# Five w2T tiles in flight, a third w1 column block loaded early, bias transposes moved and inverse tables split by engine, in a spectral mixer and token MLP with its backward pass

## The chip, the cores and the metric

The kernel runs on one core of a Trainium2 chip. A core has TensorE (PE, matmul; its weight loads are listed as PEld), VectorE (DVE), ScalarE (ACT), GpSimd (POOL) and SyncE (SP), which here issues every DMA. The metric is device time in microseconds (us). Before the change it is 399.45 us, the median of three runs (397.94 to 399.71).

## The reference

One block of a network is computed forward, and then the gradients of its output with respect to seven inputs. S = 2048 tokens, D = 448 channels, F = 1792 hidden units, bfloat16:

```
A(x)  = irfft2( rfft2(x) * (w_r + i w_i) )              # over tokens and channels
B(x)  = ( gelu( layernorm(x)^T @ w1 + b1 ) @ w2 + b2 )^T  # mixes tokens
h     = x + A(layernorm(x))
out_0 = h + B(layernorm(h))
out_1..out_7 = gradients of x, w_r, w_i, w1, b1, w2, b2 for a given grad_out
```

## The kernel before

The transforms are matmuls with tables of sines and cosines. The forward part has these stages, in the order of the trace.

**Row stage** (the loop over t in NT = 16). Block t of tokens is transformed over the channels: row_a and row_b are eight matmuls each time, with copies between them by ScalarE or VectorE. A reshape DMA (L632, one for each t, deferred by a little TensorE time) brings each result into D2, in the layout that the transform over tokens needs. Meanwhile VectorE and ScalarE build the token tables Ut and Vt from small columns made on POOL (gen_UV), and the spectral weights come in through eight row loads (w_load, L559).

**s2 stage** (s2_stage). After all sixteen reshapes VectorE negates a part of D2, and then eight column groups c2 are transformed over the tokens, multiplied by the spectral weights on VectorE (w_mult, four operations for each group) and transformed back (s2_inv). The multiplication of group c2 is emitted four steps after its transform, and the transform back two steps later still. The results go through reshape DMAs (L698) into D3. The inverse tables over channels, csI, are made by gen_inv_d, one half at the end of the row stage and one half at c2 = 1; those over tokens by gen_inv_s.

**dg filler**. A quite different product, grad_out times the transposed w2 (dg_gen, 14 tiles of 16 matmuls), is spread over the row and s2 stages to fill TensorE: fill(n) runs n of its matmuls. Each of its tiles needs a w2T tile, 512 KB, brought in by a transposing DMA (load_w2T, L292). The ring of w2T tiles has five places, three in rE and two in rO. Three tiles are loaded at the start, and when a dg tile ends, the load three tiles ahead is issued. While hold is set (from t = 2*HOLD = 14 to the start of s2) these loads are put aside and then issued at the first step of s2.

**Inverse rows** (inv_rows with h_consumer). The transform back over channels, the sum h in region rA, and its layernorm. At its end h is stored to DRAM (L926).

**GELU stage** (the loop over jp). Seven column blocks of w1, 256 columns each, are multiplied with the normalised h; GELU and its derivative follow, most of it on VectorE. The blocks come from load_w1c (L867) into a ring of three places: two in region r2, one in rA. Two are loaded before the inverse rows. The third is loaded after the h store, which reads rA.

**y stage and after**. y = gelu @ w2 with column blocks of w2 (load_w2c, L913), output (y_tail), and then the backward pass, which the change does not touch.

All orders on TensorE, ScalarE, VectorE and SyncE are the order in which the program emits instructions; POOL's are arranged by a scheduler. SyncE issues its DMAs one after the other, so each waits for the issue of all before it. Copies out of PSUM (evac) go to ScalarE or VectorE by a running count of the load of both. The bias loads put b1 and b2 into rows of smr; `turn`, deferred by 15 us of TensorE time, turns them into columns with two transposing DMAs (L759), and POOL copies them into b1col and b2col (L760). Most instructions are recorded under L78 (ScalarE and VectorE) and L212 (matmul), so the profile is read by tile names.

Of the kernel before, what the change touches and what calls it, by code (L numbers as in the profile page):

```python
# [13 lines left out]
ALU = mybir.AluOpType  # L14
# [4 lines left out]
S = 2048  # L19
# [4 lines left out]
NFB = 14  # L24
NT = 16
# [9 lines left out]
RESH_LAG = 1.1  # L35
ML_F = 4
SIDE = 2
HOLD = 7
N_FILL_F = (6, 3, 20, 3, 24, 2)
N_FILL_B = (16, 16, 40, 8, 32, 12)  # L40
INV_SD = 1.0 / float(S * D)

# [76 lines left out]
def kernel(  # L119
# [37 lines left out]
    def cut(reg, off, *dims):  # L157
        n = int(np.prod(dims))
        v = reg[:, off:off + n]
        if len(dims) == 1:  # L160
            return v
        names = "abcd"[:len(dims)]
        return v.rearrange("p (" + " ".join(names) + ") -> p " + " ".join(names),
                           **{c: d for c, d in zip(names, dims)})
# [5 lines left out]
    def ps_ff(parts=P):  # L170
        return psum.tile([P, 512], F32, tag="ff", bufs=4, name="ps_ff")
# [24 lines left out]
    def defer(us, fn, *views):  # L196
        state = [fn]

        def run():
            if state:  # L200
                state.pop()()
        later.append((clock[0] + us, len(later), run))
        later.sort(key=lambda x: x[0])
        for v in views:
            Ring.held.setdefault(id(v), []).append(run)
# [43 lines left out]
    def col(n=1):  # L249
        i = _ci[0]  # L250
        _ci[0] += n
        assert _ci[0] <= 64
        return cols[:, i:i + n]
# [33 lines left out]
    def load_w2T():  # L287
        j = w2T_ring.i
        if j == NFB:
            return  # L290
        wT = w2T_ring.next()
        nc.sync.dma_start_transpose(out=wT, in_=B_w2[j * P:(j + 1) * P, :].rearrange("f (t c) -> f t c", c=P))  # L292
        w2Ts.append(wT)
# [208 lines left out]
            mm(pt[:, i * P:(i + 1) * P], lhsT=src[:, g0 + i, :], rhs=permI[:], start=True, stop=True)  # L502
        evac(out=dst[:, g0:g0 + 4, :].rearrange("p g c -> p (g c)"), in_=pt[:])

    def gen_inv_d(ch):
        e, en = col(), col()
        gp_.memset(e, 2.0)
        if ch == 0:
            gp_.memset(e[0:1, :], 1.0)
        else:  # L510
            ve.tensor_scalar(out=e, in0=pcol, scalar1=112.0, scalar2=None, op0=ALU.not_equal)
            ve.tensor_scalar(out=e, in0=e, scalar1=1.0, scalar2=None, op0=ALU.add)
            gp_.memset(e[0:1, :], 0.0)
        ve.tensor_scalar(out=en, in0=e, scalar1=-1.0, scalar2=None, op0=ALU.mult)
        gp_.tensor_scalar(out=halves[:, ch:ch + 1], in0=e, scalar1=-0.5, scalar2=1.5, op0=ALU.mult, op1=ALU.add)
        pt = ps_ff()[:].bitcast(BF16)[:, 0:2 * 2 * P].rearrange("p (w b c) -> p w b c", w=2, b=2)
        for w in range(2):
            for b in range(2):
                nc.tensor.transpose(pt[0:KC, w, b, :], csF[:, w, b, DC * ch:DC * ch + KC], ident[:])
        for w, x in ((0, e), (1, en)):  # L520
            for b in range(2):
                lo = D - DC - DC * b
                sc.activation(out=csI[0:KC, w, ch, DC * b:DC * b + DC], in_=pt[0:KC, w, b, 0:DC], func=ACT.Copy,
                              scale=e[0:KC])
                ve.tensor_scalar(out=csI[0:KC, w, ch, lo:lo + DC], in0=pt[0:KC, w, b, DC - 1::-1], scalar1=x[0:KC],
                                 scalar2=None, op0=ALU.mult)

    base = ftmp(3072, 16, 16, 2)
    fix = ftmp(3584, 16)
# [84 lines left out]
    def row_a(t, R):  # L614
        pa = ps_ff()
        ft = folds[t // 2]
        for k in range(4):
            o = DC * (4 * (t % 2) + k)
            mm(pa[:, k * P:(k + 1) * P], lhsT=ft[:, o:o + P], rhs=R, start=True, stop=True)
        blk = blk_ring.next()  # L620
        evac(out=blk.rearrange("p a b -> p (a b)"), in_=pa[:])
        return blk
# [11 lines left out]
    def s2_stage(get_x, on_mult, ml, n_fill, gap, make_inv, after_fwd=None, scale=None):  # L634
        flush()
        for c4 in range(4):
            ve.tensor_scalar(out=D2[:, 4 * c4:4 * c4 + 4, 2, :], in0=D2[:, 4 * c4:4 * c4 + 4, 0, :], scalar1=-1.0,
                             scalar2=None, op0=ALU.mult)
        nh = NG // 2
        xs, ys = {}, {}  # L640

        def g_last(c2, i):
            return after_fwd is not None and 2 * c2 + i == NG - 1
        lag = 2 + ml
        negs.clear()
        for c2 in range(nh + lag):
            if c2 < nh:
                xs[c2] = get_x(c2)
                if make_inv and c2 < 4:
                    gen_inv_s(4 + c2)  # L650
                    if c2 == 1:
                        gen_inv_d(0)
            for i in range(2):
                if make_inv:
                    next(wp, None)
                    next(wp, None)
                if c2 < nh:
                    g = 2 * c2 + i
                    px = ps_ff()
                    pv = px[:, 0:452].rearrange("p (c k) -> p c k", c=2)  # L660
                    mm(pv, lhsT=Ut[:, g, :], rhs=D2[:, g, 1:3, :], start=True, stop=False)
                    mm(pv, lhsT=Vt[:, g, :], rhs=D2[:, g, 0:2, :], start=False, stop=True)
                    evac(out=xs[c2][:, i, :, :], in_=pv, scale=scale)
                if c2 >= lag:
                    s2_inv(2 * (c2 - lag) + i, ys[c2 - lag][:, i, :, :])
                if g_last(c2, i):
                    after_fwd()
                while negs:
                    negs.pop(0)()
                fill(n_fill)  # L670
            if ml <= c2 < nh + ml:
                ys[c2 - ml] = on_mult(c2 - ml, xs[c2 - ml])
        fill(gap)
# [78 lines left out]
    def load_biases():  # L752
        gp_.memset(smr, 0.0)
        nc.sync.dma_start(out=smr[0:NFB, 0, :], in_=B_b1.rearrange("(j p) -> j p", p=P))
        nc.sync.dma_start(out=smr[:, 1, :], in_=B_b2.rearrange("(j p) -> j p", p=P))

        def turn():
            for i, dst in ((0, b1col), (1, b2col)):
                nc.sync.dma_start_transpose(out=smc[:, i, :], in_=smr[:, i, :])  # L759
                gp_.tensor_copy(out=dst[:], in_=smc[:, i, :])  # L760
        defer(15.0, turn)


    def dg_gen():
# [30 lines left out]
    weave(fwd_c[:2], [lambda: ve.reciprocal(out=rstd_x[:, 0:4], in_=rstd_x[:, 0:4])])  # L795
    Rs = {t: scale_R(t) for t in range(2)}
    weave(fwd_c[2:])
    gp_.memset(csF[:, 0, :, 0:1], 0.0)  # L798
    ve.tensor_scalar(out=ident[:], in0=krow[:, 0:P], scalar1=pcol, scalar2=None, op0=ALU.is_equal)
    gp_.memset(W_view_F[:, :, :, DF:KW], 0.0)  # L800
    w_loads = w_load()
    uv = gen_UV()
    blks = {0: row_a(0, Rs.pop(0))}
    fold_prep(xn, 1)
    for t in (4, 5):
        ln_stats(xn, t, mvx)
    fill(N_FILL_F[0])
    load_biases()
    Meter.side, Meter.every, Meter.count = [], 1, 0
    GROUPS = {0: (4, 8), 4: (8, 12), 8: (12, 16)}  # L810
    STATS = {0: (6, 7), **{t: (t + 7,) for t in range(1, 9)}}
    INV_S = {11: 0, 12: 1, 13: 2, 14: 3}
    sc.copy(out=Rp.rearrange("p (a q b) -> p a q b", q=8, a=4), in_=Rm[:].rearrange("p (q a b) -> p a q b", q=8, a=4))
    for t in range(NT):
        hold[0] = t >= 2 * HOLD
        if t + 1 < NT:
            blks[t + 1] = row_a(t + 1, Rs.pop(t + 1))
        fill(N_FILL_F[1])
        if t + 2 < NT:
            if t + 2 in (4, 8, 12):  # L820
                while Meter.side:
                    Meter.side.pop(0)()
            Rs[t + 2] = scale_R(t + 2)
        row_b(t, blks.pop(t))
        if t % 2 and t < 12:
            fold_prep(xn, t // 2 + 2)
        for i in STATS.get(t, ()):
            ln_stats(xn, i, mvx)
        for _ in range(3 if t > 0 else 0):
            if next(uv, None):  # L830
                break
        if t in GROUPS:
            Meter.side.extend(rstd_of(*GROUPS[t]))
        if t >= 3:
            next(w_loads, None)
        if t in INV_S:
            gen_inv_s(INV_S[t])
        if t == 2:
            gen_RT()
        if t == 15:  # L840
            gen_inv_d(1)
        fill(N_FILL_F[1])
# [7 lines left out]
    def fwd_x(c2):  # L850
        hold[0] = False
        while held_w2:
            held_w2.pop(0)()
        return Xs[:, 2 * c2:2 * c2 + 2, :, :]

    def fwd_mult(c2, xc):
        return w_mult(c2, xc, W_view_F, False)

    s2_stage(fwd_x, fwd_mult, ML_F, N_FILL_F[3], N_FILL_F[4], True)

    nc.sync.dma_start(out=w_d[:], in_=rG[:, 0:NG * 2 * KW])

    w1c_ring = Ring([cut(r, o, NT, 256) for r, o in ((r2, 0), (r2, NT * 256), (rA, 0))])

    def load_w1c(jp):
        w = w1c_ring.next()
        nc.sync.dma_start(out=w, in_=B_w1.rearrange("(p t) f -> p t f", t=NT)[:, :, 256 * jp:256 * jp + 256])  # L867
        return w

    w1cs = [load_w1c(0), load_w1c(1)]  # L870

    hn = xn
    hln = cut(rB, 0, NT, 4, P)[:, :, :, 0:DC]
# [31 lines left out]
            ve.tensor_scalar(out=hln[:, t, :, :], in0=v4(hn[:, t, :]), scalar1=nmean_h[:, t:t + 1],  # L905
                             scalar2=rstd_h[:, t:t + 1], op0=ALU.add, op1=ALU.mult)

    w2c_ring = Ring([cut(r, o, NFB, 256) for r, o in ((rS, 0), (rS, NFB * 256), (r452, 0), (rO, 0), (r2, NT * 256), (r2, 0))])
    w2cs = {}

    def load_w2c(i):
# [12 lines left out]
        norm_h(t, t == 14)  # L924
    drain()
    nc.sync.dma_start(out=h_d.rearrange("(p t) d -> p t d", t=NT), in_=hn)  # L926
    w1cs.append(load_w1c(2))

    g_ = cut(rE, 0, NFB, 4, P)[:, :, :, 0:DC]
    gel = [ring(rG, i * 4 * 896, 4, 2, D) for i in range(2)]  # L930
# [279 lines left out]
```

## Time and profile before

| | |
|---|---|
| median of the runs | 399.45 us (397.94, 399.45, 399.71) |
| the profiled execution, its own time | 402.57 us |
| its span, first to last instruction | 400.8 us |
| busy share PE, DVE, ACT, POOL | 90%, 71%, 52%, 6% |
| mean granted TensorE clock | 0.982 |
| moved by DMA | 81.86 MB, 204 GB/s over the span |
| row stage, about 10 to 54 us; s2, 58 to 92; inverse rows, 97 to 116 | |
| GELU stage, 116 to 172; y stage, 172 to 216; backward, from there | |

In the views, times are microseconds from the start of the span. A timeline line gives start, duration, engine, line, operation, destination<-source, and in brackets the idle time before it with what ended it. SyncE's lines are the issues of DMAs (SPq); the transfer itself runs on 16 DMA engines and ends later. Region names that end in digits are shortened by the profile (r2, r3 and r452 all appear as r), and the tensor names too: in_B_w_dram is w1 or w2 by the line. Matmuls of 128 x 448 follow each other every 0.19 us at full clock though each is listed with some 0.35 us, as they are pipelined.

### The profile page before, as it was taken

To read this page: it belongs to the slowest core of one execution; us is meant where nothing else is said; L and a number is where in the kernel's file an instruction comes from. 1 tells how busy PE (TensorE), PEld (TensorE's weight loads), DVE (VectorE), ACT (ScalarE), POOL (GpSimd) and SP (SyncE) were. 2 spreads that over 40 slices of the span, in tenths; PEclk is the share of its full clock that TensorE was granted. 3 is DMA by queue.
4 is the path that set the end of the run, shared out by engine and by line. 5 is a ranking of instruction groups with operands and counts; after the bars stand their busy time and mean duration, and the time that the engine had idled before them with its cause. 6 is when DMAs were issued, how large, how long until landed. Compare 5 with 4: busy or idle time off the path is not lost.

```text
span 400.8 us, 6200 instructions
## 1 busy us (share of the span) xinstructions
PE 360.8 (90%) x2057; PEld 191.5 (48%) x2057; DVE 285.0 (71%) x729; ACT 207.0 (52%) x439; POOL 22.9 (6%) x92
## 2 busy tenths in 40 slices
PE   0798789988996999999999999899999889799995
PEld 0464535534643455545555666543444335455552
DVE  8979457982876588843249787737999924779784
ACT  4486455674976254414213444535545525667772
POOL 8500000000220000000030000000000000000000
PEclk9999988999999899999999999999999999999999
DMA  8979788167996999687958894596555989966775
GB/s 214 312 161 202 166 188 183 39 148 250 297 343 171 306 331 242 170 253 192 198 121 164 176 180 105 94 289 198 167 158 161 216 256 312 252 193 174 190 189 207
DMA packets 148297, 81.86 MB, mean 204 GB/s; under 512 B 97448, under 2 KB 142504, under 8 KB 147880
## 3 DMA queue, kind: packets, MB, share of 16 engines
q1 hardware_dynamic: 148264, 81.46, 80.2%
q8 instruction: 16, 0.26, 0.3%
q14 instruction: 17, 0.14, 0.1%
HBM read 27.56 MB, written 23.89 MB: 128 GB/s over the span
## 4 chain that ended last, share of the span: by engine, by line
PE 44%; DVE 26%; DMA 14%; ACT 6%; issue 5%; SPq 3%; DVEq 0%; POOL 0%; ACTq 0%
PE ps_mm L212 34%; PE ps_ff L212 10%; DVE rS L78 8%; DVE rG L78 5%; DVE r L78 4%; DMA out_dram<-r 4%; DMA rE<-in_B_w_dram 4%; DVE rO L78 3%; DMA h_d<-rA 2%; ACT rO L78 2%; DVE rD L78 2%; ACT rG L78 2%; DMA rA<-in_B_w_dram 2%; DMA out_dram<-rO 1%; SPq L292 1%
## 5 line engine op out<-in xcount | busy, mean ns | idle before, releaser
L212 PEld LDWEIGHTS <-r 128*128 128x128 bf16 (+1 forms) x596 | 57.5, 105 | 47.3 <-issue 2.9
L212 PEld LDWEIGHTS <-rst 112*128 112x128 bf16 x480 | 45.9, 98 | 53.7 <-issue 5.6
L212 PE MATMUL ps_mm<-r,rst 112*128 112x512 bf16 (+1 forms) x256 | 53.0, 356 | 5.7 <-DVE rO L78 3.1
L212 PE MATMUL ps_mm<-rG,rst 112*128 112x512 bf16 x224 | 52.9, 379 | 0.9 <-DMA rst<-rE 0.9
L78 ACT CAST rO<-ps_mm 128x512 bf16<-128x512 f32 (+1 forms) x64 | 35.0, 560 | 32.3 <-PE ps_mm L212 21.9
L212 PEld LDWEIGHTS <-rS 128*128 128x128 bf16 (+1 forms) x368 | 32.4, 99 | 36.1 <-issue 7.2
L78 DVE CAST rO<-ps_mm 128x512 bf16<-128x512 f32 (+1 forms) x56 | 35.4, 647 | 18.8 <-PE ps_mm L212 12.6
L212 PE MATMUL ps_mm<-rD,r 128*128 128x448 bf16 x224 | 44.5, 352 | 0.0
L212 PE MATMUL ps_mm<-rC,rE 128*128 128x448 bf16 x144 | 37.5, 380 | 2.9 <-DMA rE<-in_B_w_dram 2.7
L78 ACT CAST r<-ps_ff 128x452 bf16<-128x452 f32 x51 | 27.6, 540 | 13.8 <-PE ps_ff L212 13.7
L212 PE MATMUL ps_mm<-rB,r 128*128 128x448 bf16 x160 | 31.2, 352 | 0.1
L78 DVE SCALAR_TENSOR_TENSOR r<-ps_mm,b2col,r 128x448 bf16<-128x448 f32 x16 | 10.8, 682 | 22.6 <-PE ps_mm L212 16.4
L212 PE MATMUL ps_ff<-csI,rAT 113*128 113x448 bf16 x108 | 25.7, 361 | 1.2 <-ACT rAT L78 1.1
L78 ACT ACTIVATE r<-ps_mm 128x448 bf16<-128x448 f32 x16 | 8.7, 544 | 30.6 <-PE ps_mm L212 30.6
L78 ACT ACTIVATE r<-rC 128x448 bf16<-128x448 bf16 x16 | 9.1, 570 | 26.1 <-DMA out_dram<-r 19.0
L212 PE MATMUL ps_mm<-rE,rS 128*128 128x448 bf16 x112 | 21.6, 352 | 0.0
L212 PEld LDWEIGHTS <-rE 128*128 128x128 bf16 x144 | 14.1, 103 | 14.8 <-DMA rE<-in_B_w_dram 3.7
L78 ACT ACTIVATE rS<-rS 128x452 bf16<-128x452 bf16 x16 | 9.3, 581 | 22.1 <-DVE rS L78 22.1
L212 PE MATMUL ps_ff<-csF,rS 112*128 112x226 bf16 x128 | 18.6, 266 | 1.9 <-POOL csF L798 1.9
L78 DVE TENSOR_SCALAR rG<-rG 128x896 bf16<-128x896 bf16 x28 | 10.9, 389 | 12.8 <-ACT rG L78 12.8
L78 ACT ACTIVATE rG<-rG 128x896 bf16<-128x896 bf16 x14 | 13.3, 950 | 12.4 <-DVE rG L78 12.2
L212 PE MATMUL ps_mm<-rC,rO 128*128 128x448 bf16 x80 | 19.0, 353 | 0.0
(157 smaller groups left out, 571.3 us busy)
## 6 DMA issues: line engine op xcount, KB each, us to landing
r<-r SPq DMA_DIRECT2D x64, 113.0 KB
out_dram<-rO SPq DMA_DIRECT2D x14, 512.0 KB
out_dram<-rO SPq DMA_DIRECT2D x16, 448.0 KB
r<-in_B_w_dram SPq DMA_DIRECT2D x5, 1024.0 KB
rS<-in_B_w_dram SPq DMA_DIRECT2D x4, 896.0 KB
out_dram<-r SPq DMA_DIRECT2D x32, 112.0 KB
r<-in_B_w_dram SPq DMA_DIRECT2D x3, 896.0 KB
rA<-in_B_w_dram SPq DMA_DIRECT2D x2, 1024.0 KB
```

Source lines behind the costliest of these rows:

```text
L78: fn(**kw)
L212: nc.tensor.matmul(out, lhsT=lhsT, rhs=rhs, start=start, stop=stop)
L292: nc.sync.dma_start_transpose(out=wT, in_=B_w2[j * P:(j + 1) * P, :].rearrange("f (t c) -> f t c", c=P))
```

## The change

- Two more w2T loads are issued in the row loop, at t = 1 and t = 3, so that all five places of the ring are in use; from then on each finished dg tile issues the load five tiles ahead. HOLD becomes 13 and is compared with t itself. Two more filler matmuls are run ahead of s2 (22 in place of 20).
- The three inverse-table columns of each half (e, en, halves) are made by a new gen_inv_cols on POOL, ahead of gen_UV's own columns; before, VectorE made some of them inside gen_inv_d. In gen_inv_d the copies with w = 0 all go to ScalarE and those with w = 1 all to VectorE, where before each pair was split over both. The memset of csF's first column before the row stage goes from POOL to VectorE.
- load_biases returns `turn`, and s2 calls it at c2 = 4, behind the held w2T loads.
- After s2 the filler is drained, and three w1 column blocks are loaded in place of two. The third place of their ring is in rO, behind its first S columns, where two of the w2T tiles were; two w2 column blocks, which were in rO and r2, go into rA.

```
-HOLD = 7
-N_FILL_F = (6, 3, 20, 3, 24, 2)
+HOLD = 13
+N_FILL_F = (6, 3, 22, 3, 24, 2)
...
-    def gen_inv_d(ch):
+    inv_cols = {}
+
+    def gen_inv_cols(ch):
         e, en = col(), col()
+        inv_cols[ch] = (e, en)
         gp_.memset(e, 2.0)
         if ch == 0:
             gp_.memset(e[0:1, :], 1.0)
         else:
-            ve.tensor_scalar(out=e, in0=pcol, scalar1=112.0, scalar2=None, op0=ALU.not_equal)
-            ve.tensor_scalar(out=e, in0=e, scalar1=1.0, scalar2=None, op0=ALU.add)
+            gp_.tensor_scalar(out=e, in0=pcol, scalar1=112.0, scalar2=None, op0=ALU.is_equal)
+            gp_.tensor_scalar(out=e, in0=e, scalar1=-1.0, scalar2=2.0, op0=ALU.mult, op1=ALU.add)
             gp_.memset(e[0:1, :], 0.0)
-        ve.tensor_scalar(out=en, in0=e, scalar1=-1.0, scalar2=None, op0=ALU.mult)
+        gp_.tensor_scalar(out=en, in0=e, scalar1=-1.0, scalar2=None, op0=ALU.mult)
         gp_.tensor_scalar(out=halves[:, ch:ch + 1], in0=e, scalar1=-0.5, scalar2=1.5, op0=ALU.mult, op1=ALU.add)
+
+    def gen_inv_d(ch):
+        e, en = inv_cols[ch]
...
                 lo = D - DC - DC * b
-                sc.activation(out=csI[0:KC, w, ch, DC * b:DC * b + DC], in_=pt[0:KC, w, b, 0:DC], func=ACT.Copy,
-                              scale=e[0:KC])
-                ve.tensor_scalar(out=csI[0:KC, w, ch, lo:lo + DC], in0=pt[0:KC, w, b, DC - 1::-1], scalar1=x[0:KC],
-                                 scalar2=None, op0=ALU.mult)
+                for o, i_, f in ((DC * b, pt[0:KC, w, b, 0:DC], e), (lo, pt[0:KC, w, b, DC - 1::-1], x)):
+                    o = csI[0:KC, w, ch, o:o + DC]
+                    if w:
+                        ve.tensor_scalar(out=o, in0=i_, scalar1=f[0:KC], scalar2=None, op0=ALU.mult)
+                    else:
+                        sc.activation(out=o, in_=i_, func=ACT.Copy, scale=f[0:KC])
...
-        defer(15.0, turn)
+        return turn
...
-    gp_.memset(csF[:, 0, :, 0:1], 0.0)
+    nc.vector.memset(csF[:, 0, :, 0:1], 0.0)
...
     uv = gen_UV()
+    gen_inv_cols(0)
+    gen_inv_cols(1)
...
-    load_biases()
+    turn_biases = load_biases()
...
     for t in range(NT):
-        hold[0] = t >= 2 * HOLD
+        hold[0] = t >= HOLD
+        if t in (1, 3):
+            load_w2T()
...
             held_w2.pop(0)()
+        if c2 == 4:
+            turn_biases()
         return Xs[:, 2 * c2:2 * c2 + 2, :, :]
...
     s2_stage(fwd_x, fwd_mult, ML_F, N_FILL_F[3], N_FILL_F[4], True)
+    drain()
...
-    w1c_ring = Ring([cut(r, o, NT, 256) for r, o in ((r2, 0), (r2, NT * 256), (rA, 0))])
+    w1c_ring = Ring([cut(r, o, NT, 256) for r, o in ((r2, 0), (r2, NT * 256), (rO, S))])
...
-    w1cs = [load_w1c(0), load_w1c(1)]
+    assert not pending
+    w1cs = [load_w1c(jp) for jp in range(3)]
...
-    w2c_ring = Ring([cut(r, o, NFB, 256) for r, o in ((rS, 0), (rS, NFB * 256), (r452, 0), (rO, 0), (r2, NT * 256), (r2, 0))])
+    w2c_ring = Ring([cut(r, o, NFB, 256) for r, o in ((rS, 0), (rS, NFB * 256), (r452, 0), (rA, 0), (rA, NFB * 256), (r2, 0))])
...
     nc.sync.dma_start(out=h_d.rearrange("(p t) d -> p t d", t=NT), in_=hn)
-    w1cs.append(load_w1c(2))
```

## The prediction

> **What bounds the kernel now.** The profiled execution took 402.57 us, its span is 400.8 us. I read the chain that ended last first. Three of its pieces lie where the change works:
>
> ```profile
> 43.16 5.16 DMA rE<-in_B_w_dram
> ...
> 53.70 3.43 DMA r<-r
> ...
> 115.49 7.85 DMA h_d<-rA
> 123.41 6.18 DMA rA<-in_B_w_dram
> ```
>
> These are a w2T tile that TensorE waits for, the last reshape before the s2 stage, and the h store with the third w1 column block behind it (the block's buffer is the region the store reads). The matmul timeline prices them; the bracket is idle time and what ended it:
>
> ```profile
> 48.36 0.97 PE L212 MATMUL ps_mm<-rC,rE 128*128 128x448 bf16 x3 [2.33 <-DMA rE<-in_B_w_dram]
> ...
> 57.90 0.36 PE L212 MATMUL ps_ff<-r,Ut 128*128 128x452 bf16 x1 [1.94 <-DVE r L78]
> ...
> 129.64 7.91 PE L212 MATMUL ps_mm<-rB,rA 128*128 128x448 bf16 x32 [3.02 <-DMA rA<-in_B_w_dram]
> ```
>
> Idle TensorE before s2 is not yet a bound, so I read SyncE's issue timeline (start, duration):
>
> ```profile
> 20.70 2.27 SPq L292 DMA_TRANSPOSE rO<-in_B_w_dram  x1
> ...
> 25.95 3.99 SPq L292 DMA_TRANSPOSE rO<-in_B_w_dram  x1
> ...
> 33.23 3.15 SPq L292 DMA_TRANSPOSE rE<-in_B_w_dram  x1
> ...
> 39.31 2.48 SPq L759 DMA_TRANSPOSE smc<-rst  x2
> ...
> 43.16 3.06 SPq L292 DMA_TRANSPOSE rE<-in_B_w_dram  x1
> ...
> 48.99 2.46 SPq L292 DMA_TRANSPOSE rE<-in_B_w_dram  x1
> 51.55 2.77 SPq L632 DMA_DIRECT2D r<-r  x4
> 54.41 4.88 SPq L292 DMA_TRANSPOSE rO<-in_B_w_dram  x2
> ```
>
> From 18.4 to 66.7 us each issue begins within 0.13 us of the end of the last: the queue never rests. Row 12 leaves TensorE at about 41 us, and its reshape (first of the x4) is issued at 51.55. So s2 starts when SyncE reaches the sixteenth reshape (53.70) and that lands 3.43 us later, not when TensorE is done. The view of waits lists L292 as waiting for TensorE, 9.4 us in its largest entry; but a slot was last read two tiles earlier, and the timeline has no gap. I trust the timeline.
>
> The windows view of the GELU stretch shows the other bound:
>
> ```profile
> 130.00:135.00 5.00, 5.00 (x20) 2.22 (x18) 4.12 (x11) 1.39 (x2) 0.00 (x0) 0.66 1.20 290
> 135.00:140.00 5.00, 5.00 (x28) 2.57 (x27) 1.33 (x6) 1.78 (x3) 0.00 (x0) 1.00 1.19 315
> ```
>
> Columns: busy PE, PEld, DVE, ACT, POOL, then granted clock, DMA share, GB/s. VectorE, with 6.54 us of work per column block, runs dry at 135-140: the late third block reaches it late. From 139.24 to 171.98 it is full (five blocks in 32.7 us).
>
> **What the Trainium skill says.** "Perfetto Trace Analysis", section What "DMA-bound" means: a kernel can be bound on the issuing engine's sequencer, seen as a track solid with DMA slices. Here it is: 48 us without a rest. "DMA: Bandwidth & Descriptors", Issuing engines are not separate DMA queues: issue time is usually small beside the transfer. Here a tile's issue (2.27 us) is about as long as its transfer, so it isn't. "TensorE: Matmul & The Clock Gate", Part 1: an idle window of about 3.4 us puts the array at half clock. The trace agrees: after the 3.02 us wait 32 matmuls took 7.91 us, against 6.22 us for a later block.
>
> **The change, part by part.**
>
> *1. Forward queue.* Tiles 3 and 4 are loaded at t = 1 and 3, and later loads come two tiles earlier. So seven w2T loads, not five, stand before the sixteenth reshape (issue order of the changed kernel: seven, then four behind it; before, five, then six). HOLD 13 in place of 2*7 holds the same tiles, since no tile ends between the two. The two bias transposes leave this stretch. Price of an added load: the first cost 2.27, three back to back at the start of s2 7.26, so 2.35 with an issue gap 2.4. Two are +4.8; the biases are -2.53 with gaps: +2.3. One load then follows three W row loads directly where 2.48 us of biases used to separate it, and the load that does so now cost 3.99 where others cost 2.27: I add 0.3 of that. Sum **+2.6 us**. Bounds: the four stretched loads have 3.58 us above 2.27 in all; should it all vanish, the sum is -1.3; should both added ones cost 3.99, it is +5.5. Behind the queue stand the reshapes, for them VectorE's negation of D2, for that all of s2. All of it moves.
>
> *2. The 2.33 us TensorE stall* goes, because tile 6 now arrives some 8 us before use. It pays nothing: what is late next is the reshape, already the later of the two. The same holds for the 1.93 us that TensorE waits at 16.20 for the csF memset now moved from POOL to VectorE: tile 1 lands at 18.84 in either kernel. TensorE idles longer ahead of s2, some 7 to 8 us. Its clock was half for 3.4 us already after the 1.94 us wait (0.51 in 58.88-62.30), a loss of 1.7. It can now be anything from 0.8 to 2.5 by the phase of the window: **0, -0.9 to +0.8**.
>
> *3. Bias transposes in s2.* SyncE there rests from 66.69 to 74.49 before the first inverse reshape; the four tiles left and 2.48 us of biases fit. The last two loads need tiles 7 and 8 used up, which falls inside this rest. First use of b1col is at 119.85. **0**; without that cover 2.5 us on the reshapes.
>
> *4. Inverse tables.* In s2, ACT and VectorE alternate over eight pieces, 61.77 to 64.53; apart they are 4 x 0.36 and 4 x 0.29. TensorE's waits that follow are 0.38 and 0.26, so at most -0.6. Against it, the load balance moves: VectorE takes ten of the sixteen spectrum copies in place of six, one of them (0.63) directly ahead of the first spectral multiply. **0, -0.6 to +0.6.** POOL gets six more column operations of 0.2 to 0.4 us ahead of the U/V chain that ends at 16.1; VectorE first needs its last column at 18.43: hidden, unless they take over 2.3. The csF memset costs VectorE 0.1 there.
>
> *5. Fill.* Two matmuls move from the gap behind s2 to the idle stretch ahead of it: 2 x 0.19 = **-0.4**. The drain ahead of the w1 loads finds nothing left (6 + 96 + 22 + 84 of 224 matmuls are done, and the gap has room for 24 more).
>
> *6. Third block.* It now queues behind the first two, at about 101 us, into rO. One more 1 MB keeps the saturated DMA engines (about 290 GB/s) busy 3.6 us longer, to 119; no engine waits for these loads. The h store lands about 3 us later, near 126; behind it on SyncE stand the fourth w2 block (needed in the y stage) and the fifth w1 block, due at about 142 and landed by 135. VectorE then starts the third block right after the second: 128.98 + 6.54 = 135.52 in place of 139.24, **-3.7**. TensorE gains 3.0 of wait and 1.7 of half clock, 4.7, so VectorE sets it. What follows is handed on whole: y_tail(0) at 172.11 waits for VectorE, then TensorE runs without a gap. Bounds -3.0 to -4.2.
>
> Sum: 2.6 + 0 + 0 + 0 - 0.4 - 3.7 = **-1.5 us**, 401.1 for the profiled execution. Its 402.57 lies 3.1 above the median of the runs, 399.45; the same difference puts the median at **398.0**.
>
> **Rivals.** *The queue absorbs it.* Tiles 3 to 5 are now issued ahead of the W rows, and the DMA engines have room (share 0.83 over 20-54). If part 1 is 0, the sum is -4.1: 395.4. For it: the DMA engines were nearly idle at 20-22. Against: the time is in SyncE's serial issues, and two were added.
>
> *The forward stage is bound by transfers, not issues: slower.* If every tile behind the pause costs what the one behind the W rows did, 3.99, the two added ones cost 8.0 less 2.5, and three others stretch by 0.84, 0.93 and 1.53: +8.8 in place of 2.6. Sum +4.7: 404.1. The forecast turns to slower beyond +6.1 in part 1. For it: DMA share 0.99 over 30-40. Against: 0.71 over 40-50.
>
> *The third block doesn't pay.* If the stall moves to the fourth or fifth block behind the late h store, part 6 is worth 1.0: 400.7. Against: 7 us of margin.
>
> **How the numbers follow.** About 0.5% (2.0 us) is what a measurement of this kernel can tell from no change: below 397.45 is faster, above 401.45 slower. Chances: the forecast 0.58, absorbed 0.20, transfer-bound 0.10, no pay 0.12. The forecast's own spread is 396.2 to 399.8 (parts 1, 2 and 4); 0.17 of its 0.58 lie below 397.45. Faster: 0.17 + 0.19 = 0.36; slower: 0.10 + 0.04 = 0.14; within: 0.50. The range 395.2 to 401.3 leaves out the transfer-bound case and the tails.
>
> **What would show it.** Right: SyncE solid until the sixteenth reshape, issued at 56-57 with seven tile loads ahead; no w2T wait, but 4 us or more idle ahead of s2; the third block continuous behind the second; everything after the GELU stage 1 to 2 us earlier. Wrong: the sixteenth reshape at or before 54 or after 60, or VectorE still dry in the third block.

## The result and the profile after

The changed kernel is slower. In the first comparison its median is 402.71 us (401.60 to 404.15) against 398.77 us (397.94 to 399.71), a ratio of 1.010 with an interval of 1.0057 to 1.0143. A repeat on a second chip, with 22 runs of it, gave 1.0039 (1.0022 to 1.0057). So it loses 1.6 us by the narrower measurement and up to 3.9 us by the first; which of the two is nearer I can't say. The forecast was 398.0, with 401.3 as the upper end. All ratios here leave out executions more than 1.5% above the fastest of the same kernel, so they can differ a little from the quotient of the medians given beside them.

The profiled execution took 404.15 us, its span is 402.4 us. I profiled the kernel before a second time too ("before again", below), so that each side has two executions. The stages then compare like this (means of two, us):

| from ... to | before | after | difference |
|---|---|---|---|
| start ... first s2 matmul | 58.37 | 63.22 | +4.85 |
| ... first csI matmul of the inverse rows (the s2 stage) | 40.53 | 39.98 | -0.55 |
| ... first GELU | 21.69 | 21.69 | 0 |
| ... first y_tail (the GELU stage) | 52.03 | 48.54 | -3.49 |
| ... end | 228.02 | 228.80 | +0.78 |
| span | 400.64 | 402.23 | +1.59 |

The last row of stages is spread, not change: over all profiled executions of this study that stretch took between 225.4 and 229.3 us.

SyncE's issue timeline of the changed kernel (start, duration) answers the one of before:

```profile
19.73 1.92 SPq L292 DMA_TRANSPOSE rO<-in_B_w_dram  x1
...
22.58 2.14 SPq L292 DMA_TRANSPOSE rO<-in_B_w_dram  x1
...
25.54 3.27 SPq L292 DMA_TRANSPOSE rE<-in_B_w_dram  x1
...
31.09 3.94 SPq L292 DMA_TRANSPOSE rE<-in_B_w_dram  x1
...
38.33 3.35 SPq L292 DMA_TRANSPOSE rE<-in_B_w_dram  x1
...
45.91 5.01 SPq L292 DMA_TRANSPOSE rO<-in_B_w_dram  x1
...
53.69 3.06 SPq L292 DMA_TRANSPOSE rO<-in_B_w_dram  x1
56.85 2.75 SPq L640 DMA_DIRECT2D r<-r  x4
```

There are seven tile loads ahead of the x4, as forecast, and no bias transposes. But where the first two loads took 1.92 and 2.14 us to issue, the sixth took 5.01 for the same 512 KB. The seven sum to 22.69 us; the five of before to 14.93. That is +7.76 for two added loads that I had priced at 4.8. The sixteenth reshape, last of the x4, is issued at 58.99 instead of 53.70. The chain that ended last goes through exactly this:

```profile
53.69 3.06 SPq L292
...
58.99 3.55 DMA r<-r
...
63.28 0.93 PE ps_ff L212 x2
```

The matmul timeline shows s2's first matmuls, and the third w1 block (in rO) in the GELU stage:

```profile
63.28 0.56 PE L212 MATMUL ps_ff<-r,Ut 128*128 128x452 bf16 x1 [11.27 <-DVE r L78]
63.64 0.58 PE L212 MATMUL ps_ff<-r,Vt 128*128 128x452 bf16 x1
...
121.05 10.79 PE L212 MATMUL ps_mm<-rB,r 128*128 128x448 bf16 x55
131.68 4.51 PE L212 MATMUL ps_mm<-rB,rO 128*128 128x448 bf16 x23
```

TensorE now stands still for 11.27 us ahead of s2 (1.94 before), and the matmuls there take 0.56 and 0.58 where they take 0.35 at full clock. The third block starts with no wait in brackets; the 3.02 us are gone. The windows view (busy PE, PEld, DVE, ACT, POOL, then granted clock, DMA share, GB/s) has both ends of the story, first the forward stretch, then the GELU windows that answer the two shown of before:

```profile
20.00:54.00 34.00, 30.21 (x233) 18.99 (x231) 24.56 (x87) 23.09 (x47) 0.11 (x1) 1.00 0.97 183
...
131.00:136.00 5.00, 5.00 (x28) 2.57 (x27) 4.38 (x11) 2.30 (x3) 0.00 (x0) 1.00 1.12 304
136.00:141.00 5.00, 5.00 (x29) 2.60 (x27) 4.56 (x11) 2.34 (x4) 0.00 (x0) 1.00 1.21 307
```

VectorE is busy 4.38 and 4.56 of 5 us in the third block, where it had run down to 1.33: the dry stretch is gone. And the DMA engines were busy for 0.97 of the forward stretch. Before it was 0.83, at nearly the same rate of bytes (178 and 183 GB/s), so the longer queue of loads did not raise the rate by much:

```profile
20.00:54.00 34.00, 29.86 (x220) 18.54 (x218) 24.18 (x88) 21.59 (x45) 0.71 (x5) 0.95 0.83 178
```

### The profile page after: what moved, and what is told of

The parts are those of the page before. It is cut to its first block, busy times and chain, and to the rows that moved or that the text cites. A ratio compares the mean times of both kernels' runs of the same rounds, so it can differ in the third digit from the quotient of the medians.

```text
span 402.4 us, 6200 instructions
## 1 busy us (share of the span) xinstructions
PE 357.4 (89%) x2057; PEld 190.7 (47%) x2057; DVE 285.3 (71%) x727; ACT 207.0 (51%) x438; POOL 22.2 (6%) x95
## 2 busy tenths in 40 slices
DMA packets 148297, 81.86 MB, mean 203 GB/s; under 512 B 97448, under 2 KB 142504, under 8 KB 147880
## 4 chain that ended last, share of the span: by engine, by line
PE 43%; DVE 28%; DMA 12%; ACT 7%; issue 5%; SPq 4%; DVEq 0%; ACTq 0%; POOL 0%
PE ps_mm L212 33%; PE ps_ff L212 10%; DVE rS L78 9%; DVE rG L78 6%; DVE r L78 4%; DMA out_dram<-rO 3%; DMA out_dram<-r 2%; DMA rE<-in_B_w_dram 2%; DVE rO L78 2%; ACT rG L78 2%; DMA r<-r 2%; DVE rD L78 2%; SPq L292 2%; ACT rO L78 2%; DMA rX<-in_A_x_dram 1%
## 5 line engine op out<-in xcount | busy, mean ns | idle before, releaser
L212 PEld LDWEIGHTS <-r 128*128 128x128 bf16 (+1 forms) x568 | 54.7, 106 | 44.8 <-issue 3.0
L212 PE MATMUL ps_mm<-rC,rE 128*128 128x448 bf16 x144 | 36.5, 373 | 2.4 <-DMA rE<-in_B_w_dram 2.4
L78 ACT CAST r<-ps_ff 128x452 bf16<-128x452 f32 x49 | 26.5, 542 | 9.6 <-PE ps_ff L212 6.5
L212 PE MATMUL ps_ff<-r,Ut 128*128 128x452 bf16 x32 | 12.0, 376 | 12.4 <-DVE r L78 12.4
L212 PEld LDWEIGHTS <-rO 128*128 128x128 bf16 (+1 forms) x165 | 15.8, 99 | 13.0 <-issue 0.9
```

What stands on the lines that cost most here:

```text
L78: fn(**kw)
L212: nc.tensor.matmul(out, lhsT=lhsT, rhs=rhs, start=start, stop=stop)
```

## The experiments

Two theories stood against each other. **I** is the forecast's: the forward stretch is bound by SyncE's serial issues, each with its own price. **T** is its rival: it is bound by what the DMA engines carry, and an issue on SyncE takes as long as the engines behind it make it take. The expectations of the first four runs write Q and M for the two readings of how much of the early third block arrives at the end.

| run | ahead of the sixteenth reshape: w2T tiles, biases | reshape issued, us | s2 stage, us | ratio to before, interval |
|---|---|---|---|---|
| before; before again | 5, yes | 53.70; 54.37 | 40.26; 40.79 | |
| early third block | 5, yes | 55.45 | 39.20 | 0.9935 (0.9916 to 0.9955) |
| tables only | 5, yes | 53.66 | 37.92 | 0.9968 (0.9942 to 0.9994) |
| biases back | 5, yes | 54.84 | 37.95 | 0.9869 (0.9833 to 0.9906) |
| three tiles | 5, no | 54.37 | 38.21 | 0.9896 (0.9865 to 0.9926) |
| one held | 4, yes | 53.05 | 42.60 | 0.9958 (0.9928 to 0.9987) |
| four tiles | 6, no | 56.45 | 40.16 | 0.9967 (0.9943 to 0.9992) |
| five only | 7, yes | 57.65 | 40.91 | 1.0159 (1.0113 to 1.0204) |
| after; after again | 7, no | 58.99; 58.52 | 40.10; 39.86 | 1.0100; 1.0039 |
| old tables | 7, no | 59.86 | 40.91 | 1.0084 (1.0052 to 1.0116) |
| warm | 7, no | 58.60 | 37.75 | 0.9912 (0.9877 to 0.9946) |

The s2 stage is counted from its first matmul to the first csI matmul of the inverse rows; the inverse rows open with twelve matmuls with RTm, 1.1 to 2.8 us before that one. Ratios are against runs of the kernel before on the same chip; four chips served the runs after the first comparison, so two ratios from different chips are compared with some caution.

**Early third block alone.** The kernel before with the third part of the change only:

```
-    w1c_ring = Ring([cut(r, o, NT, 256) for r, o in ((r2, 0), (r2, NT * 256), (rA, 0))])
+    w1c_ring = Ring([cut(r, o, NT, 256) for r, o in ((r2, 0), (r2, NT * 256), (rO, S))])
...
-    w1cs = [load_w1c(0), load_w1c(1)]
+    w1cs = [load_w1c(jp) for jp in range(3)]
...
-    w1cs.append(load_w1c(2))
```

> The kernel before with the early third w1 block alone (third place of its ring in rO, two w2 blocks in rA). Theory Q (the forward DMA queue costs 5.3 us by the two profiled spans, the third block gives 3.8 back): 3.7 us faster than before, 395.1; VectorE starts the third block right behind the second. Rival M (the medians lost 2.3 us more than the profiled executions did, because the third block gives back less in an ordinary execution): 1.4 us faster, 397.4.

Measured: 398.86 us beside 401.76, ratio 0.9935, so -2.6 us (-1.8 to -3.4). In the profiles, first GELU to first y_tail takes 48.54 us. Every kernel here whose third block comes early has 48.5, the two executions of before have 52.3 and 51.8. So this stage gains 3.3 to 3.7 us, as forecast. The profiled span is 3.4 us below the mean of the two of before; the run times show somewhat less. In this execution the sixteenth reshape came 1 to 2 us later than before's, for no reason that I found.

**Three tiles.** The whole change without its two added loads:

```
-HOLD = 13
+HOLD = 14
...
-        if t in (1, 3):
-            load_w2T()
```

> The changed kernel without the two extra w2T loads (three tiles in flight, HOLD 14), all else kept. Theory Q: five tile loads and no bias transposes ahead of the sixteenth reshape, which is issued at 51 to 52 us; against the changed kernel 7.8 us come back (5.3 net and the 2.5 of the biases), some 395. Rival M: 5.3 come back at most in the forward part, but the loss behind s2 stays: 397 to 398.

Measured: 397.09 us, ratio 0.9896. The kernel gains what the other parts bring, and is faster than the kernel before and the changed one. But the reshape came at 54.37, not at 51 to 52: taking the 2.5 us of biases out of the queue bought nothing. SyncE's timeline of this run says why:

```profile
40.97 5.24 SPq L292 DMA_TRANSPOSE rE<-in_B_w_dram  x1
...
49.36 2.77 SPq L292 DMA_TRANSPOSE rE<-in_B_w_dram  x1
52.23 2.76 SPq L640 DMA_DIRECT2D r<-r  x4
```

The load that stood behind the biases in the kernel before, where it took 3.06 us, follows the W row loads directly here, and takes 5.24. What left the queue came back as a longer issue. This was the first run that spoke against theory I.

**Five only.** The kernel before with five tiles in flight and 22 fillers, biases in place:

```
-HOLD = 7
-N_FILL_F = (6, 3, 20, 3, 24, 2)
+HOLD = 13
+N_FILL_F = (6, 3, 22, 3, 24, 2)
...
-        hold[0] = t >= 2 * HOLD
+        hold[0] = t >= HOLD
+        if t in (1, 3):
+            load_w2T()
```

> The kernel before with five tiles in flight alone (loads at t = 1 and 3, HOLD 13, fill 22), biases in their old place. Theory Q: seven tile loads and the biases ahead of the sixteenth reshape, issued near 61 us; 7 to 8 us slower than before, 406 to 407. Rival M: 5 us slower, 404.

Measured: 407.56 us, ratio 1.0159, the slowest of all: +6.4 us for the two loads and two fillers alone (its profiled span, 404.1, shows 3.5 of them). The reshape is issued at 57.65, earlier than in the changed kernel (58.99), although two transposes more stand ahead of it.

**W rows from ScalarE.** The changed kernel with the eight W row loads on ScalarE's queue:

```
-                nc.sync.dma_start(out=W_rows[p0:p1, c_, j0:j1, :],
+                nc.scalar.dma_start(out=W_rows[p0:p1, c_, j0:j1, :],
```

> The changed kernel with its eight W row loads issued by ScalarE in place of SyncE: the same bytes, but SyncE has eight issues less and the tiles no row loads ahead of them in its own queue. If the forward stretch is bound by SyncE's serial issue: the sixteenth reshape is issued near 46 us, s2 starts when TensorE and VectorE are done, near 52 to 54, and the time falls by 8 us or more, to 394 or below. If it is bound by the transfers (DMA share 0.97 over 20 to 54 us): the tile issues stretch as before, the sixteenth reshape at 56 to 58, the time within 2 us of the changed kernel.

Measured: 404.76 us, ratio 1.0036 (1.001 to 1.0063), like the changed kernel. Eight issues fewer stand on SyncE ahead of the x4 and the reshape still came late, at 63.39 (this execution lay 3 us above its median, so I read only its order of events). Tile loads still stretch, to 5.58 and 4.71 us, with no row load ahead of them in SyncE's own queue. It decides less than I had hoped: ScalarE is now held by its loads, 5.01 us in one place, and with it the copies of the row stage.

**W rows with a sixteenth of the bytes.** This is the clean form of the same question: all issues at their places, and only the bytes gone.

```
-                nc.sync.dma_start(out=W_rows[p0:p1, c_, j0:j1, :],
+                nc.sync.dma_start(out=W_rows[p0:p1, c_, j0:j0 + 1, :],
...
-                                              [[P * DF, 16]] + dims + [[1, (j1 - j0) * DF]]))
+                                              [[P * DF, 16]] + dims + [[1, DF]]))
```

The placing step reads that one row, broadcast over four groups.

> The changed kernel with the eight W row loads issued as before and at the same places, but each fetching one of the up to sixteen rows per partition (about a sixteenth of their bytes); the placing step reads that one row for all. It leaves out most of the spectral weights, so what it computes is not the reference. Theory T (the forward stretch is bound by what the DMA engines carry): the stretched tile issues (5.01, 3.94 us) fall to about 3, the sixteenth reshape is issued at 52 to 55 instead of 58.99, and the kernel gets faster than before by 3 to 6 us. Theory I (bound by the serial issues of SyncE, each with its own price): the tile issues and the reshape stay within 1 us of the changed kernel (58 to 59), the time within 1 us of it.

Measured: 396.88 us, ratio 0.9839 (0.9792 to 0.9885). SyncE's timeline:

```profile
43.53 2.02 SPq L292 DMA_TRANSPOSE rO<-in_B_w_dram  x1
...
48.32 2.40 SPq L292 DMA_TRANSPOSE rO<-in_B_w_dram  x1
50.82 2.75 SPq L640 DMA_DIRECT2D r<-r  x4
```

The load that took 5.01 us takes 2.02, and the reshape is issued at 52.95 instead of 58.99, 6.0 us earlier. The DMA share over 20 to 54 fell from 0.97 to 0.80, which is 5.8 us of all 16 engines (0.17 x 34). The same instructions stand in the same order, and the whole run moves as many packets (148,297 in all), but 1.7 MB less. That settles it for T: the long issues were time in which SyncE waited for the DMA engines. It also hints at the other limit: most issues are left with about 2 us (one still took 3.83), and the queue is still solid. With fewer bytes still, the issues would be the bound; no run shows that.

**Biases back.** Three tiles, with the bias transposes back in the forward stretch:

```
-        return turn
+        defer(15.0, turn)
...
-        if c2 == 4:
-            turn_biases()
```

> Three tiles in flight with the rest of the change, and the bias transposes put back into the forward stretch, where they hold the queue of SyncE for 2.5 us. Theory I: the sixteenth reshape moves from 54.37 to about 57, the time 2.5 us above that of three tiles alone (ratio about 0.996 against before). Theory T: the transfers catch up during the pause, the next tile issue falls from 5.24 to about 3, the reshape stays at 54 to 55.5, the ratio at 0.989 to 0.992.

Measured: 398.7 us, ratio 0.9869; the reshape at 54.84. SyncE's timeline, to be set beside the one of three tiles:

```profile
39.95 2.48 SPq L767 DMA_TRANSPOSE smc<-rst  x2
...
43.81 3.48 SPq L292 DMA_TRANSPOSE rE<-in_B_w_dram  x1
...
50.06 2.53 SPq L292 DMA_TRANSPOSE rE<-in_B_w_dram  x1
52.69 2.76 SPq L640 DMA_DIRECT2D r<-r  x4
```

The load behind the biases takes 3.48 where it took 5.24 without them: 2.48 us of issue cost 0.47 us at the reshape. The biases were a pause in which the engines caught up, not a cost. Its ratio and that of three tiles overlap; it has the lowest ratio of the versions here that compute everything, about 5 us faster than before.

**The changed kernel again.**

> The changed kernel as it is, for a ratio beside the other runs of this chip. If the loss is what the profiled executions show, the ratio is 1.004 (1.6 us); if it is what the medians showed, 1.010 (3.9 us).

Measured: 405.22 us beside 403.44, ratio 1.0039, with the stage times of the table. The first comparison's 3.9 us did not come again.

**Four tiles.** The changed kernel with one of its two added loads (`if t == 1`).

> The changed kernel with one of its two extra w2T loads: four tiles in flight, six tiles ahead of the sixteenth reshape. Theory T, one tile's transfer each: the reshape at 56 to 57, halfway between 54.37 (three tiles) and 58.99 (five), TensorE's idle time ahead of s2 5 to 6 us, the ratio about 1.000. If the loss came only with the half clock after an idle time above some length, the ratio lies near one end (0.990 or 1.010) and not between.

Measured: 402.21 us, ratio 0.9967; the reshape at 56.45, 2.1 above three tiles and 2.1 to 2.5 below five. Each tile costs about the same there. The ratio falls between too, so the loss is not the half clock alone. Part of the first step is, though: from three tiles to four s2 starts 1.9 us later and, now at half clock, takes 1.95 us longer; from four to five it starts 1.9 to 2.0 us later and takes no longer.

**Tables only.** The three tiles and biases-back runs had reached the inverse rows 1.3 and 1.9 us ahead of the early third block, though they start s2 within 0.6 us of it. What was left were the tables:

```
+    gen_inv_cols(0)
+    gen_inv_cols(1)
...
-                sc.activation(out=csI[0:KC, w, ch, DC * b:DC * b + DC], in_=pt[0:KC, w, b, 0:DC], func=ACT.Copy,
-                              scale=e[0:KC])
-                ve.tensor_scalar(out=csI[0:KC, w, ch, lo:lo + DC], in0=pt[0:KC, w, b, DC - 1::-1], scalar1=x[0:KC],
-                                 scalar2=None, op0=ALU.mult)
+                    if w:
+                        ve.tensor_scalar(out=o, in0=i_, scalar1=f[0:KC], scalar2=None, op0=ALU.mult)
+                    else:
+                        sc.activation(out=o, in_=i_, func=ACT.Copy, scale=f[0:KC])
```

> The kernel before with the inverse tables made in the new way (columns on POOL ahead of the forward stage, csI split by engine, one memset moved), nothing else. Forecast N, as in the prediction: 0 within 0.6 us, ratio 0.998 to 1.002. Rival P: three tiles and biases-back both reached the inverse stage 1.3 to 1.9 us ahead of the early third block alone, which they differ from by these tables and two fill steps; if the tables did it, the ratio is 0.995 to 0.997.

Measured: 401.32 us, ratio 0.9968, so -1.3 us (-0.2 to -2.3): P, not N. VectorE's timeline of the kernel before, then ScalarE's (idle time and its releaser in brackets):

```profile
62.16 0.28 DVE L78 TENSOR_SCALAR csI<-ps_ff,cols 113x112 bf16<-113x112 bf16 x1 [0.51 <-ACT csI L78]
```

```profile
62.47 0.35 ACT L78 ACTIVATE csI<-ps_ff,cols 113x112 bf16<-113x112 bf16 x1 [0.34 <-DVE csI L78]
```

and the same of tables only, VectorE and then ScalarE:

```profile
61.80 0.83 DVE L78 TENSOR_SCALAR csI<-ps_ff,cols 113x112 bf16<-113x112 bf16 x4
```

```profile
60.68 1.09 ACT L78 ACTIVATE csI<-ps_ff,cols 113x112 bf16<-113x112 bf16 x4
```

Before, the two engines took turns, each waiting for the other, and both were held from 61.77 to 64.54. Now four follow four, and each engine gives only its own 0.83 or 1.09 us; behind each other on one engine four cost less than four times one. All eight read one PSUM tile, and the Trainium skill, "PSUM — Partial Sum Buffer", section PSUM bank collisions raise a hardware error, says that two engines may not be in the same partitions of one bank at the same time. The traces agree: the two do not overlap here, in either kernel. So the split by engine did not make them parallel; it took away six of the seven turns.

But that is not where the time was won. Up to the first RTm matmul, the s2 stage is no shorter with the new tables than with the old (the table under part 2 below). The gain comes right behind it, where the first csI matmul waits for ScalarE's copies (rAT). ScalarE of the kernel before, then TensorE:

```profile
95.60 0.53 ACT L78 CAST rD<-ps_mm 128x448 bf16<-128x448 f32 x1 [3.44 <-PE ps_mm L212]
96.13 1.28 ACT L78 ACT_TABLE_LOAD   x1
...
97.54 1.06 ACT L78 CAST rAT<-ps_ff 113x512 bf16<-113x512 f32 x2
```

```profile
98.16 0.93 PE L212 MATMUL ps_ff<-csI,rAT 113*128 113x448 bf16 x4 [1.08 <-ACT rAT L78]
```

and of tables only VectorE, ScalarE and TensorE:

```profile
94.32 0.62 DVE L78 CAST rD<-ps_mm 128x448 bf16<-128x448 f32 x1 [3.34 <-PE ps_mm L212]
```

```profile
91.83 1.28 ACT L78 ACT_TABLE_LOAD   x1
...
95.40 1.07 ACT L78 CAST rAT<-ps_ff 113x512 bf16<-113x512 f32 x2 [2.07 <-PE ps_ff L212]
```

```profile
96.04 0.93 PE L212 MATMUL ps_ff<-csI,rAT 113*128 113x448 bf16 x4 [0.23 <-ACT rAT L78]
```

evac gave the copy of the last dg tile (rD) to ScalarE before, and gives it to VectorE here: the tables' edit takes small operations off VectorE and reorders others, and so shifts the running count of load. On ScalarE that copy stands ahead of a load of its function table, 1.28 us, and the rAT copies come behind both. On VectorE it lets the table load be over before the rAT copies are due. All sixteen profiled executions sort by this copy: with it on ScalarE (before twice, early third block, five only, old tables, one held, held warm) the first csI matmul waits 1.08 to 1.93 us, with it on VectorE (the other nine) 0.23. One held and held warm have the new tables and still wait 1.93, so it is the copy and not the way the tables are written. No run moves the copy alone.

The s2 stage fell by 2.6 us from the mean of the two of before: 1.6 up to the first RTm matmul, where this execution happened to have full clock, and 1.0 behind it, the copy. By the runs 1.3 reach the end. The GELU stage takes 53.92 us instead of 52.03, for the third block is as late as ever:

```profile
129.31 7.78 PE L212 MATMUL ps_mm<-rB,rA 128*128 128x448 bf16 x32 [4.82 <-DMA rA<-in_B_w_dram]
```

It arrives at 129.31 (129.64 before), and TensorE waits 4.82 us instead of 3.02.

**Old tables.** The changed kernel with the tables of before.

> The changed kernel with the inverse tables made in the old way. N: as the changed kernel on this chip, ratio to before about 1.004. P: 1.3 to 1.9 us slower than the changed kernel, ratio 1.007 to 1.009.

Measured: 405.52 us, ratio 1.0084 against 1.0039, so 1.8 us slower than the changed kernel: P again, but weakly. The two intervals just touch (1.0022 to 1.0057 and 1.0052 to 1.0116), the chips differ, and beside the first comparison's 1.0100 nothing would be left. Its profile says where time goes. The last dg copy is on ScalarE again (a wait of 1.37 us), and the s2 stage is 0.9 us longer (40.91 and 39.98). The inverse rows behind it, from the first csI matmul to the first GELU, take 23.21 us instead of 21.69, for the granted clock is 0.50 in 107 to 109. Five only, with the old tables too, has the same 23.21.

**Warm.** The changed kernel with matmuls put into the idle time ahead of s2:

```
     fill(N_FILL_F[2])
+    pd = ps_mm()
+    for k in range(45):
+        mm(pd[:, 0:448], lhsT=go_tp[:, k % NT, 0:P], rhs=go_tp[:, k % NT, 0:D], start=(k == 0), stop=(k == 44))
```

> The changed kernel with 45 extra 128x448 matmuls, whose result nobody reads, at the end of the forward stage, where TensorE has nothing to do (8.5 us at full clock in 9 to 11 us of idle time). Theory C: the half clock after the idle time costs what separates the two lengths of the s2 stage, 40.1 and 38.2 us; with the array kept busy the first s2 matmuls take 0.35 instead of 0.58 us a pair of records, the stage 38 to 38.5 us, the kernel 1.5 to 2 us less than the changed one (ratio about 0.999). Rival: the stage has slack elsewhere, its length stays at 40, the ratio at 1.004.

Measured: 398.94 us, ratio 0.9912. The matmul timeline:

```profile
51.77 8.68 PE L212 MATMUL ps_mm<-rC 128*128 128x448 bf16 x45
...
63.31 0.36 PE L212 MATMUL ps_ff<-r,Ut 128*128 128x452 bf16 x1 [2.64 <-DVE r L78]
63.51 0.35 PE L212 MATMUL ps_ff<-r,Vt 128*128 128x452 bf16 x1
```

s2 starts when it did in the changed kernel (63.28), at full clock, and takes 37.75 us instead of 39.98. So the half clock costs 2.2 us, and 45 useless matmuls take it back. The ratio says 5.1 us, on another chip than the 1.0039; in the profile the rest lies in the backward pass of this execution (first y_tail to end 225.4 us, 228.8 in the changed kernel), which the matmuls do not touch. I have no cause for that.

**Before again.**

> The kernel before, profiled on the chip of these runs, so that its milestones can be set beside theirs. If its profiled execution of the first chip was typical, the sixteenth reshape is issued at 53.2 to 54.2 and the s2 stage takes about 40 us; if it lay at the slow end, the stage takes 38 to 39 us and the span is 2 to 4 us shorter than 400.80.

Measured: 402.25 us, span 400.5, reshape at 54.37, s2 stage 40.79. The first profile was typical, though its own time lay 3.1 us above the first median.

**One held.** Does the price of a tile also hold downwards? Biases back, with the fifth tile kept until s2 begins, and so with fewer fillers ahead of s2:

```
-HOLD = 14
-N_FILL_F = (6, 3, 22, 3, 24, 2)
+HOLD = 12
+N_FILL_F = (6, 3, 8, 3, 24, 2)
```

> Biases-back with one w2T tile fewer ahead of the sixteenth reshape (four, HOLD 12): the fifth is held until s2 begins, and the filler ahead of s2 is cut from 22 to 8 matmuls, since its tile is not there. Theory T with a price for each tile: the reshape is issued at 52 to 53 instead of 54.84. If s2 follows it, the ratio to before falls from 0.987 to 0.982 to 0.984. Rival S: three tiles was already at the point where something else sets s2 (TensorE waits longer, filler that is missing), and time stays or rises: ratio 0.987 or more.

Measured: the reshape at 53.05, 1.8 earlier, and s2 started 2.2 earlier (56.85). But the ratio is 0.9958: slower than biases back. The matmul timeline shows what is late instead:

```profile
58.73 0.36 PE L212 MATMUL ps_mm<-rC,rE 128*128 128x448 bf16 x1 [0.94 <-DMA rE<-in_B_w_dram]
...
90.45 3.38 PE L212 MATMUL ps_mm<-rC,rE 128*128 128x448 bf16 x17
93.66 3.19 PE L212 MATMUL ps_mm<-rC,rO 128*128 128x448 bf16 x16
...
99.45 0.93 PE L212 MATMUL ps_ff<-csI,rAT 113*128 113x448 bf16 x4 [1.93 <-ACT rAT L78]
```

TensorE waits for the held tile inside s2, and 33 fillers are left behind s2 where biases back has 16 in one block; the inverse rows wait for them, and then 1.93 us for a copy by ScalarE. The first csI matmul comes 2.5 us later than in biases back (99.45 and 96.98), and 1.7 of that is this wait: the last dg copy is ScalarE's again. So T holds for the reshape and S for the time, but most of the loss is the copy's, and what a fourth load alone would bring in time is not shown.

**Held and warm.** The same with 14 matmuls for the 14 fillers that were cut.

> One tile held, with 14 matmuls whose result nobody reads in place of the 14 fillers that were cut. If a longer idle time ahead of s2 puts the first s2 matmuls of one-tile-held at half clock, this run takes 1.5 to 2 us less than it; if not, the same within 0.8 us.

Measured: 397.64 us, ratio 0.9931 (0.9906 to 0.9956) beside 0.9958 (0.9928 to 0.9987): the intervals overlap, so nothing can be told.

## Why the prediction was wrong

**Part 1, the forward queue, is the step that failed.** It forecast +2.6 us and the reshape at 56 to 57; +4.85 was measured at the first s2 matmul, with the reshape at 58.5 to 59. Of its terms, the credit of 2.53 for the biases is the one that was wrong: it was 0. With five tiles, five executions of four kernels with the biases ahead have the reshape at 53.7 to 55.5, and the one without has it at 54.37. The price of 4.8 for the two added tiles came near in size, but by luck, for it was the price of an issue in a queue that the issues did not bound. The tiles cost 2.1 to 2.3 us each without the biases (54.37 to 58.52 and 58.99) and 1.6 with them (54.4, the mean of the five, to 57.65), and nothing pays it back. What I read as a bound, SyncE without a rest for 48 us, was partly SyncE waiting for the engines behind it. The Trainium skill, in "Perfetto Trace Analysis", section What "DMA-bound" means, takes a solid sequencer track for descriptor generation and not data movement; here the measurement decides against it, since the same issue fell from 5.01 to 2.02 us when other loads lost their bytes. "DMA: Bandwidth & Descriptors", section Issuing engines are not separate DMA queues, fits: all run on the same 16 engines, and the W rows from ScalarE brought nothing. The rival had this mechanism right and its size wrong (+8.8); I gave it 0.10 because of a DMA share of 0.71 over 40 to 50. That window held part of the bias transposes: it was the pause that they made, and not room to spare. In the changed kernel the same ten microseconds have 1.08, in three tiles 1.09, in biases back 0.84.

**Part 2** held. The 2.33 us stall went and paid nothing. The half clock was said to cost 0 more (-0.9 to +0.8). The s2 stage up to the first RTm matmul sorts by it:

| first s2 matmul to first RTm matmul, us | full clock at its start | half clock within 1.1 us of its start |
|---|---|---|
| tables of before | 36.60 | 38.33, 38.60, 38.53, 38.69 |
| tables of the change | 37.13, 36.87, 36.84, 36.66 | 39.01, 38.78, 39.08, 38.62 |

The row of before has the early third block at full clock, and before, before again, five only and old tables at half. The row of the change has three tiles, biases back, tables only and warm at full clock, and after, after again, four tiles and W rows with a sixteenth of the bytes at half. (One held and held warm, whose filler differs, and W rows from ScalarE are left out.) Half clock costs 1.9 us with the old tables and 2.0 with the new, so it had been paid before, and the change added nothing that these executions can tell. "TensorE: Matmul & The Clock Gate", Part 1, names an idle window of about 3.4 us. The changed kernel agrees: after 11.27 us of idle time the matmuls took 0.56 to 0.58 us, and the warm kernel's 0.35. The kernel before had half clock after idle times of 1.94 and 2.24 us, which are shorter.

**Part 3** held: 0. Where the biases stand makes no difference that the ratios of three tiles and biases back show.

**Part 4** was wrong too, by a smaller amount. It gave the tables 0 (-0.6 to +0.6); the ratios say -1.3 and -1.8. The two waits of TensorE that I priced, 0.38 and 0.26, are gone in tables only, but by the first RTm matmul nothing of that is left. I saw that the load balance moves and counted it as a cost, in the spectrum copies of s2; I did not follow it to the end of s2, where it takes the last dg copy off ScalarE. The wait behind that copy fell from 1.08 and 1.33 us to 0.23. That is also the whole of the -0.55 in the s2 stage of the first table: -0.98 from the first RTm to the first csI matmul, and +0.43 ahead of it.

**Part 5** (-0.4) was not measured by itself. **Part 6** held: -3.7 forecast, -3.5 measured, with the third block continuous behind the second.

With the measured terms the sum is 4.85 - 0.55 - 3.49 = +0.8, and with the 0.8 of spread in the rest the +1.6 of the profiles. The sign of the result hangs on part 1, and within it on the credit for the biases: without it the forecast's own sum is +1.0.

## What to carry to other kernels

That a queue of issues never rests does not show that the issues bound it. Compare the shortest with the longest issue of one kind (2.0 and 5.0 us here): if they differ, ask what the DMA engines carry at that time, and give no credit for a short transfer that leaves the queue. A prefetch that removes a wait is charged to whatever stands behind it in the same queue, so look first for what is due next there. And where a running count deals out copies to two engines, a small edit can move a copy that stands far from it: before you credit an edit, look at who does the copies behind it.

## What was unexpected of the hardware

- The issue time of a 512 KB transposing load on SyncE varies with what other DMAs carry at that time: 1.9 to 2.4 us at best, up to 5.2 among the W row loads of SyncE's queue, and 5.58 with these on ScalarE's.
- An idle time of about 2 us ahead of s2 gave half clock in both executions of before (1.94 and 2.24 us) and full clock in tables only (2.01 us) and warm (2.64 us); its length alone does not tell which.
- A function table load of 1.28 us on ScalarE cost TensorE nothing or 0.9 to 1.7 us here, by which engine had the one copy ahead of it (a wait of 0.23 us, or of 1.08 to 1.93).
- The DMA share of a stretch is not work alone: over 20 to 54 three tiles has 0.95 and the kernel before 0.83, with the same loads but for the biases. Here a share of 0.7 or 0.8 did not tell that the engines had room.
